# Moving eleven of the sixteen sums behind the gradient of b2 into three units of the first pass

## The chip, the cores and the metric

The kernel runs on one core of a Trainium2 chip. The core's engines are TensorE (PE, the matmuls), VectorE (DVE), ScalarE (ACT), GpSimd (POOL) and SyncE (SP, which only issues transfers); each works through its own instructions in the order in which the program gives them, and semaphores tie the engines together. The metric is the device time of one execution in microseconds (us).

## The reference

A forward pass of two branches mixed by a gate, and the gradients of all its inputs but one. `x` has 2048 tokens of 1024 features, and the hidden layer of the second branch has 3584.

```python
g = sigmoid((x * gate_w).sum(-1, keepdims=True))
X = rfft2(x.astype(float32)) * (w_r + 1j * w_i)
a = irfft2(X, s=(S, D)).astype(bfloat16)
h = einsum("bsd,df->bsf", B_x, w1) + b1
r = where(h > 0, h, 0)
b = einsum("bsf,fd->bsd", r * r, w2) + b2
out = g * a + (1 - g) * b
...
_out, _vjp = jax.vjp(_f, A_x, A_w_r, A_w_i, B_w1, B_b1, B_w2, B_b2, gate_w)
return (_out, *_vjp(grad_out))
```

The gradient at the second branch's output is `db = (1 - g) * grad_out`, a matrix of 2048 tokens by 1024 features. The gradient of `b2` is the sum of `db` over the tokens. The same `db`, multiplied by `w2` turned around, gives the gradient at the hidden layer.

## The kernel before

The second branch runs in three passes. The first pass (`mlp_in`) makes the hidden layer and its gradient and writes both to memory (`h2T_scr`, `dhT_scr`). The second (`mlp_grads`) makes the gradients of `w1` and `w2`, the third (`Outputs`) the output and the gradient of `x`. Beside the first two passes runs the first branch, a transform in stages written as generators: `first_stage` (rows, then columns of the forward transform), `fft_mid` (the rest of it, the filters, their gradients, the first part of the way back), `fft_out`. The function `spread` advances them: after each step of the pass it takes as many steps of the transform as are due. In the first pass that is 1.75 per step until `fft_mid` has begun (`"mid" in later`) and 1.5 after it. So the order of the program is fixed when the kernel is built; a list scheduler then gives each engine's final order.

The first pass begins with a stretch over the first 512 of the 3584 hidden columns. After it come 23 *units*, numbered here from 0. A unit (`Unit(fp, sp)`) is 256 hidden columns by 1024 tokens. It makes its part of the hidden layer by seven products (`p1` to `p7`, line 927, four matmuls of 512 columns each, on sums that VectorE prepares: `w_sums`, line 916). VectorE and ScalarE take these apart (`rest`: line 946 on VectorE joins two products into `rT`; line 947 is ScalarE's relu; line 934 are ScalarE's copies `cu` and `u2`; line 794 squares). Each unit also does four `back_` of the unit before: eight matmuls with `w2T` and `dbT` into a bank `pd` (line 826), and one VectorE instruction that makes `dhT` from it (line 830). The PSUM banks of `pd` and `pZ` come from one pair, those of `ph` from another; a product can start only when VectorE or ScalarE has read the one before last out of its bank. The transform's banks come from a third pair (tag `ps2`).

A unit has four steps, each ended by a `yield`: the first with `p1`, a `back_` and `p5`, the second with `p6` and a `back_`, the third with `p7` and a `back_`, the fourth with a `back_`, `p4`, `p3` and the next unit's `p2`.

The transform's lines that the text names: the first stage folds on VectorE (lines 272 to 284), matmuls `pk` (293) and `pu` (325), and joins `u` (312, 313); the middle stage reads `z` from memory (line 404, issued by ScalarE, and 402), mirrors it (`pm`, `z`, 426), multiplies matrices `px` (435), copies `x` (443 to 445), multiplies by the filter `tt` (453), joins `y` (458), makes the filter's gradient `g`, `gs` (500, 501; `gw`, 505), and goes back through `pv` (472) and `pc` (488, 489). POOL brings the filter into order (`w`, 410 to 417) and issues most stores. Before the middle stage's first product, the lines at the edges are made by `edges_through`: `parted` (357), `pe`, `ed` (366 to 370), `sp`, `ex` (382).

`dbT` holds `db` with the features on the partitions: eight chunks of 128 features, each with its 2048 tokens along the row. A sum over the tokens is a VectorE reduction along the row; `sum_of_db(n)` (line 991) does one half of one chunk, 1024 tokens, and there are sixteen of them. Each is placed behind the latest `dhT` instruction in VectorE's order (`later["last"]`), without a semaphore. `grad_of_b2` adds the two halves (line 996), turns the result by one PE transpose (line 998) into a `ps2` bank, copies it (line 1000) and stores it (line 1001). Before the change, units 1 to 16 make one sum each, in their fourth step, and unit 17 calls `grad_of_b2`.

Of the kernel before, what the change touches and what calls it, by code (L numbers as in the profile page):

```python
# [141 lines left out]
def kernel(  # L142
# [30 lines left out]
    S2, DC, FC = g.S2, g.DC, g.FC  # L173
# [76 lines left out]
    def after(ins, earlier, wait=mybir.DependencyClass.Sync):  # L250

        if earlier is not None:
            info = mybir.DependencyInfo(wait, mybir.DependencyReason.DATA)
            tc.add_manual_dep(ins.ins, earlier.ins.name, info, reason="paced")
# [514 lines left out]
    def mlp_in():  # L769
# [52 lines left out]
        def grads(fc, sb, ss, rT, dhT):  # L822
            w_ = w2T[fc // FGC]
            pd = d_bank("pd")
            for ec in range(DC):
                turn["PE"] = mm(  # L826
                    pd[:], lhsT=w_[:, ec, fc % FGC * P : (fc % FGC + 1) * P], rhs=dbT[:, ec, ss],
                    start=(ec == 0), stop=(ec == DC - 1),
                )
            return STT(  # L830
                out=dhT, in0=pd[:], scalar=2.0, in1=rT, op0=ALU.mult, op1=ALU.mult,
                accum_out=gb1part[:, fc, sb : sb + 1],
            )

        def load_w2(fg, earlier=None, halves=(0, FGW // 2)):

            if fg not in w2T:
                w2T[fg] = wb.tile([P, DC, FGW], BF16, name="w2T", tag="w2T", bufs=2)
            for h in halves:
                f0 = fg * FGW + h  # L840
                after(turned(w2T[fg][:, :, h : h + FGW // 2], B_w2[f0 : f0 + FGW // 2, :]), earlier)
# [5 lines left out]
        def load_w1(fp):  # L847
            w1[fp] = f1.tile([P, DC, PW], BF16, name="w1f", tag="w1f") if fp == 2 else wb.tile([P, DC, PW], BF16, name="w1g", tag="w1g", bufs=2)
            ld(out=w1[fp][:], in_=w1v[:, :, fp * PW : (fp + 1) * PW])
# [6 lines left out]
        def store(scr, t_, fp, sp):  # L856
            cols2 = slice(2 * sp * SW, 2 * (sp + 1) * SW)
            st(out=scr[2 * fp : 2 * fp + 2, :, cols2].rearrange("c p s -> p c s"), in_=t_[:])  # L858
# [18 lines left out]
        def back_(fp, s, c):  # L877
            if (fp, s // 2) not in dh:
                dh[fp, s // 2], left_of[fp, s // 2] = wide("dhT"), 4
            last = grads(2 * fp + c, s, rows_(s), rTs.pop((fp, s, c)), dh[fp, s // 2][:, c, rows_(s % 2)])  # L880
            later["last"] = last
            left_of[fp, s // 2] -= 1
            if not left_of[fp, s // 2]:
                store(dhT_scr, dh.pop((fp, s // 2)), fp, s // 2)
# [23 lines left out]
        def w_sums(fp, tie=None):  # L908
            (a11, a12), (a21, a22) = w_quads(fp)
            if fp % 2:  # L910
                s_ = kept[:, NT - 2 : NT, :].rearrange("p t (n f) -> p (t n) f", f=P).rearrange("p (q n) f -> p q n f", q=4)
            else:
                s_ = wb.tile([P, 4, KH, P], FP16, name="Sw", tag="Sw", bufs=1)
            s1, s2, s3, s4 = (s_[:, n] for n in range(4))
            for out, x, y, op in ((s1, a21, a22, ALU.add), (s2, s1, a11, ALU.subtract), (s3, a11, a21, ALU.subtract), (s4, a12, s2, ALU.subtract)):
                after(V(out=out, in0=x, in1=y, op=op), later["last"] if tie else None, mybir.DependencyClass.NoSync)
                yield
            S_[fp] = {1: s1, 2: s2, 3: s3, 4: s4}
# [70 lines left out]
        def sum_of_db(n):  # L989
            ec, h = divmod(n, 2)  # L990
            summed = nc.vector.reduce_sum(out=gb2[:, ec, h : h + 1], in_=dbT[:, ec, h * S // 2 : (h + 1) * S // 2], axis=mybir.AxisListType.X)
            after(summed, later["last"], mybir.DependencyClass.NoSync)

        def grad_of_b2():
            whole = wb.tile([P, DC], BF16, name="gb2b", tag="gb2b")
            V(out=whole[:], in0=gb2[:, :, 0], in1=gb2[:, :, 1], op=ALU.add)
            pb = fps.tile([DC, P], BF16, name="pb2", tag="ps2", bufs=2)
            nc.tensor.transpose(pb[:], whole[:], identb[:])
            row = wb.tile([DC, P], BF16, name="gb2r", tag="gb2r")
            nc.vector.tensor_copy(out=row[:], in_=pb[:])  # L1000
            st(out=out_7.rearrange("(c p) -> c p", p=P), in_=row[:])
# [31 lines left out]
        def freed_rows(n, low, high):  # L1033
            if n == freed + 1:
                again(slice(2 * low, 2 * low + 2), later["last"])
            elif n == len(seq) - 1 and high:
                again(slice(6 + 2 * high, 8 + 2 * high))

        units_ = [Unit(*u) for u in seq]
        first = [(i, k) for i in range(2) for k in range(2)]  # L1040
        units_[0].p2()
        for n, u in enumerate(units_):
            fg, pr = divmod(u.fp, NPR)
            if (u.fp, u.sp) == (LAST - 2, 1):
                load_w1(LAST)
            elif u.sp == 0 and u.fp < LAST - 1:
                load_w1(u.fp + 1)
            u.p1()
            if n:
                units_[n - 1].square(0, u.copy)  # L1050
            back_(*waiting[0])
            u.p5()
            freed_rows(n, 0, 1)
            if first and u.sp and "mid" in later and u.fp >= FC // 4:
                turned_group(0, *first.pop(0), later["last"])
            yield
            next(more_sums, None)
            u.p6()
            freed_rows(n, 1, 2)
            if n:  # L1060
                units_[n - 1].square(1, u.copy)
            back_(*waiting[1])
            next(more_sums, None)
            follows = u.fp + 1 if u.sp == 1 and u.fp < LAST - 2 else {(LAST - 2, 0): LAST - 1, (LAST - 1, 1): LAST}.get((u.fp, u.sp))
            ahead_ = w_sums(follows, True) if follows else iter(())
            dealt = ahead_ if (u.fp, u.sp) != (LAST - 2, 0) else iter(())
            next(dealt, None)
            yield
            u.p7()
            back_(*waiting[2])  # L1070
            next(more_sums, None)
            next(dealt, None)
            freed_rows(n, 2, 0)
            yield
            back_(*waiting[3])
            for _ in ahead_:
                pass
            next(more_sums, None)
            if pr == 0 and u.sp == 0:
                later["blocks"] = later["last"]  # L1080
            if 0 < fg < FG - 1 and pr == 0 and u.sp == (fg > 2):
                load_w2(fg + 1, later["last"])
            if 0 < n <= 2 * DC:
                sum_of_db(n - 1)
            elif n == 2 * DC + 1:
                grad_of_b2()
            u.p4()
            freed_rows(n, 3, 3)
            u.p3()
            if n + 1 < len(units_):  # L1090
                units_[n + 1].p2()
            yield
            waiting = [(u.fp, 2 * u.sp + j, c) for c, j in ((0, 0), (0, 1), (1, 1), (1, 0))]
# [14 lines left out]
    def group(n):  # L1108
        return later["odd" if n % 2 else "even"][:].rearrange("p (t f) -> p t f", t=NT)

    def turned_group(n, i, k, earlier):
        scr, fg = (h2T_scr, dhT_scr)[n // FG], n % FG
        rows_ = scr[:].rearrange("c p s -> (c p) s")[fg * FGW + i * FGW // 2 : fg * FGW + (i + 1) * FGW // 2]
        tiles, f_ = slice(k * NT // 2, (k + 1) * NT // 2), slice(i * FGW // 2, (i + 1) * FGW // 2)
        after(turned(group(n)[:, tiles, f_], rows_[:, k * S // 2 : (k + 1) * S // 2]), earlier)

    def again(rows_, earlier=None):
        after(ld(out=dbn[:, rows_, :], in_=db_scr[:, rows_, :]), earlier)
# [703 lines left out]
    warm(7)  # L1822

    units = mlp_in()
    rows_of_x(0, 2)
    vrow = f1.tile([FC + DC, P], BF16, name="vrow", tag="vrow")
# [143 lines left out]
```

## Time and profile before

| | us |
|---|---|
| median of 3 runs (1190.86 to 1193.34) | 1192.29 |
| the profiled execution, its own time | 1196.52 |
| its span, first to last instruction | 1194.7 |
| PE busy | 1173.5 |
| VectorE busy | 897.9 |
| ScalarE busy | 531.0 |
| POOL busy | 387.9 |
| the 16 sums of line 991, together | 19.4 |

The sums start at 111.5, 128.6, 147.2, 161.4, 178.8, 195.8, 209.8, 223.2, 238.8, 253.9, 268.5, 283.7, 298.7, 313.4, 330.0 and 345.1 us. They last 1.205 to 1.216 us each, and none of them has VectorE idle in front of it. The first pass's last products lie at about 455 us. The clock granted to PE is 1.00 in every stretch.

In the views shown below, a line of the timeline has the start in us, the duration, the engine, the line of the kernel, the operation, what it writes and reads, its shape, and how many instructions are merged in it; in brackets stand the idle time of the engine before it and what ended that. In a table of stretches, a row has the stretch, its length, and for each engine the busy time and the number of instructions, then PE's clock, the share of the transfer engines and GB/s. "issue" is idle time for which the profile shows no wait.

### The profile page before, as it was taken

The page shows a single profiled execution, that of the slowest core. Times are in us where ns is not written, and L with a number is a line of the kernel's source. Part 1 is how long each engine was busy: PE and PEld are TensorE (multiplying, and loading weights), DVE is VectorE, ACT ScalarE, POOL GpSimd, SP SyncE. Part 2 cuts the span into 40 slices and gives each one's busy share as a digit, 9 for nine tenths or more (in the row PEclk, how much of TensorE's full clock was granted, in tenths as well). Part 3 has the DMA queues.
Part 4 walks back from the last instruction along what each step waited for, and adds up shares of the span by engine and source line. Part 5 has one row for each costly group of instructions (what it writes and reads, how often), then busy time and mean ns, then how long its engine had stood idle before and what let it go on. Part 6 is the DMA issues. An engine that isn't in the chain of part 4 may idle for free.

```text
span 1194.7 us, 19383 instructions
## 1 busy us (share of the span) xinstructions
PE 1173.5 (98%) x7181; PEld 640.3 (54%) x7275; DVE 897.9 (75%) x1598; ACT 531.0 (44%) x961; POOL 387.9 (32%) x618
## 2 busy tenths in 40 slices
PE   8999999999999999999999999999999999999998
PEld 5555555444433444444446999998544444444444
DVE  6898887788988797877537666676786777976757
ACT  5678788577676773445224665664210010000000
POOL 0233443556666683764231333221001100000000
PEclk9999999999999999999999999999999999999999
DMA  9997675687979879889997999995889998564530
GB/s 264 287 306 215 187 203 167 196 219 180 206 186 198 253 250 184 200 187 219 208 198 165 238 226 251 243 216 153 258 188 267 238 277 272 176 194 149 180 124 36
DMA packets 329464, 249.84 MB, mean 209 GB/s; under 512 B 187912, under 2 KB 287658, under 8 KB 328858
## 3 DMA queue, kind: packets, MB, share of 16 engines
q1 hardware_dynamic: 268352, 112.12, 45.1%
q0 software_dynamic: 35136, 111.72, 29.6%
q10 hardware_dynamic: 25882, 24.76, 7.1%
q8 instruction: 57, 0.93, 0.3%
q14 instruction: 37, 0.30, 0.1%
HBM read 114.82 MB, written 89.67 MB: 171 GB/s over the span
## 4 chain that ended last, share of the span: by engine, by line
PE 69%; DVE 16%; DMA 5%; ACT 4%; issue 4%; POOL 1%; SPq 1%; ACTq 0%; another core or an unknown queue 0%; DVEq 0%; POOLq 0%
PE pX L1256 15%; PE xX L1557 14%; PE pV L1256 11%; PE pd L826 8%; PE xV L1557 7%; PE ph L927 4%; PE xZ L1557 3%; PE ph L819 2%; DVE rT L946 2%; DVE dhT L830 1%; DVE tt L453 1%; PE pui L325 1%; PE pki L634 1%; DMA z<-z_scr 1%; PE pu L325 1%
## 5 line engine op out<-in xcount | busy, mean ns | idle before, releaser
L826 PE MATMUL pd<-dbT,w2T 128*128 128x512 bf16 x860 | 206.5, 379 | 7.8 <-DVE rT L946 2.5
L826 PEld LDWEIGHTS <-w2T 128*128 128x128 bf16 x896 | 86.3, 98 | 110.4 <-issue 10.3
L1557 PEld LDWEIGHTS <-dS 128*128 128x128 f16 x686 | 66.4, 98 | 79.4 <-issue 3.8
L830 DVE SCALAR_TENSOR_TENSOR dhT<-pd,rT 128x512 bf16<-128x512 f32 x112 | 76.6, 684 | 31.6 <-PE pd L826 29.2
L1608 POOL DMA_DIRECT2D out_dram<-ot x32 | 17.4, 544 | 248.6 <-DVE ot L1664 128.0
L1674 ACT ACTIVATE w2br<-w2br,dsc 128x512 f32<-128x512 bf16 x8 | 5.8, 723 | 178.6 <-DVE ot L1664 117.4
L1557 PE MATMUL xX<-oT,dS 128*128 128x512 f16 x336 | 76.4, 379 | 0.6 <-DVE eR L1586 0.5
L1272 ACT COPY u<-pX 128x512 f32<-128x512 f32 x56 | 32.8, 586 | 90.8 <-PE pX L1256 85.2
L1557 PEld LDWEIGHTS <-odd 128*128 128x128 bf16 (+1 forms) x462 | 44.8, 98 | 51.5 <-issue 0.9
L1557 PEld LDWEIGHTS <-even 128*128 128x128 bf16 (+1 forms) x448 | 43.6, 98 | 52.6 <-issue 0.7
L1256 PEld LDWEIGHTS <-T 128*128 128x128 f16 x672 | 64.6, 98 | 7.5 <-issue 0.2
L947 ACT ACTIVATE rT<-rT 128x512 bf16<-128x512 bf16 x69 | 43.4, 629 | 50.2 <-DVE rT L946 49.8
L794 ACT ACTIVATE h2T<-rT 128x1024 bf16<-128x1024 bf16 x56 | 59.6, 1064 | 0.2
L1276 DVE TENSOR_TENSOR whi<-pV,u 128x512 bf16<-128x512 f32 x28 | 19.3, 689 | 47.1 <-ACT u L1272 47.0
L1256 PEld LDWEIGHTS <-S 128*128 128x128 f16 x336 | 32.5, 98 | 40.8 <-DVE S L1188 1.9
L491 POOL DMA_DIRECT2D y_scr<-pc x64 | 47.2, 738 | 18.1 <-DVE pc L488 11.1
L453 DVE TENSOR_TENSOR tt<-x,w 128x1028 f16<-128x1028 f16 (+1 forms) x64 | 42.6, 699 | 10.5 <-ACT x L445 4.5
L1256 PEld LDWEIGHTS <-resL 128*128 128x128 bf16 x448 | 43.1, 98 | 4.9
L1256 PEld LDWEIGHTS <-resR 128*128 128x128 f16 (+1 forms) x448 | 42.9, 98 | 4.9 <-issue 0.2
L1276 DVE TENSOR_TENSOR wlo<-pV,u 128x512 bf16<-128x512 f32 x28 | 19.2, 687 | 32.0 <-PE pV L1256 31.9
L858 POOL DMA_DIRECT2D h2T_scr<-h2T x28 | 20.9, 746 | 66.9 <-ACT f L285 29.2
L239 POOL DMA_DIRECT2D r<-y_scr x48 | 28.0, 588 | 41.9 <-ACT re L613 33.1
(382 smaller groups left out, 2798.0 us busy)
## 6 DMA issues: line engine op xcount, KB each, us to landing
h2T_scr<-h2T POOLq DMA_DIRECT2D x28, 512.0 KB, 4.3
dhT_scr<-dhT POOLq DMA_DIRECT2D x28, 512.0 KB, 6.0
y_scr<-pc POOLq DMA_DIRECT2D x64, 128.0 KB, 4.3
ax_scr<-yo POOLq DMA_DIRECT2D x16, 512.0 KB, 5.1
out_dram<-ot POOLq DMA_DIRECT2D x31, 256.0 KB, 3.7
z<-z_scr ACTq DMA_DIRECT2D x60, 128.0 KB, 4.2
out_dram<-whi POOLq DMA_DIRECT2D x28, 256.0 KB, 4.9
out_dram<-wlo POOLq DMA_DIRECT2D x28, 256.0 KB, 5.6
```

The lines of the kernel that those rows point to most:

```text
L239: st(out=a, in_=b) if stored else st(out=b, in_=a)
L453: V(out=tt[:, k, :, :, 0:W], in0=x[:, a : a + 2, :, 0:W], in1=by, op=ALU.mult)
L491: st(out=columns_of(y_scr, c, h), in_=pc[:, n])
L794: after(nc.scalar.activation(h2T, rT, ACT.Square), behind_, mybir.DependencyClass.NoSync)
L826: turn["PE"] = mm(pd[:], lhsT=w_[:, ec, fc % FGC * P : (fc % FGC + 1) * P], rhs=dbT[:, ec, ss], start=(ec == 0), stop=(ec == DC - 1),)
L830: return STT(out=dhT, in0=pd[:], scalar=2.0, in1=rT, op0=ALU.mult, op1=ALU.mult, accum_out=gb1part[:, fc, sb : sb + 1],)
L927: turn["PE"] = mm(acc[:], lhsT=lhs[:, t, :], rhs=rhs[:, t, :], start=start and t == 0, stop=t == KH - 1, skip_group_check=True,)
L947: nc.scalar.activation(rT, rT, ACT.Relu)
L1256: self.mm = mm(out, lhsT=lhs[:, t, m * P : (m + 1) * P], rhs=rhs[:, t, :], start=start and t + a == 0, stop=t == KH - 1, skip_group_check= ...
L1272: turn["ACT"] = nc.scalar.copy(out=t_[:], in_=self.X[:])
L1276: turn["DVE"] = self.added = V(out=self.half(row, j), in0=self.sums(acc), in1=self.sums(t_), op=ALU.add)
L1557: ins = mm(acc, lhsT=lhs[:, fc, :], rhs=rhs[:, fc, :], start=start and fc == 0, stop=fc == KH - 1 and bias is None, skip_group_check=True,)
```

## The change

A list holds the sixteen sums that are left, and `db_sum` makes the next one where its condition holds. The fourth step of a unit makes one from unit 1 on, as before; the first three steps make one each from unit 6 on. So units 1 to 5 make one sum each, units 6 and 7 four each, unit 8 the last three, in its first three steps. `grad_of_b2` is called at the head of the fourth step of unit 10 in place of unit 17. First stage and middle stage of the transform meet in units 7 and 8. What is computed stays the same.

```diff
+        db_left = list(range(2 * DC))
+
+        def db_sum(now):
+            if now and db_left:
+                sum_of_db(db_left.pop(0))
+
         units_[0].p2()
         for n, u in enumerate(units_):
...
             if first and u.sp and "mid" in later and u.fp >= FC // 4:
                 turned_group(0, *first.pop(0), later["last"])
+            db_sum(n >= 6)
             yield
             next(more_sums, None)
             u.p6()
...
             next(dealt, None)
+            db_sum(n >= 6)
             yield
             u.p7()
             back_(*waiting[2])
...
             freed_rows(n, 2, 0)
+            db_sum(n >= 6)
             yield
+            if n == 10:
+                grad_of_b2()
             back_(*waiting[3])
...
-            if 0 < n <= 2 * DC:
-                sum_of_db(n - 1)
-            elif n == 2 * DC + 1:
-                grad_of_b2()
+            db_sum(n > 0)
             u.p4()
```

In the order that the scheduler makes of it, the eleven sums stand on VectorE between the `dhT` instructions of units 6, 7 and 8, and `grad_of_b2`'s transpose on PE stands after the first `pv` of the middle stage and ahead of the `px` that follows it. PE's order differs by a few matmuls passed by others; from the end of the sums' old places on, the engines' orders are the same as before. On SP's queue one load of `w1g` stands ahead of two transposing loads of `w2T` that it stood behind.

## The prediction

> **What bounds the kernel now.** First the page's busy times, then a table of stretches cut at the sums of line 991, then TensorE's own pauses, the chain of waits, and the order in which VectorE works around one sum. I number the units from 0 as the loop does; unit n made sum n-1 in its fourth step, so the stretch that ends at a sum's start is one unit.
>
> ```profile
> span 1194.7 us, 19383 instructions
> ...
> PE 1173.5 (98%) x7181; PEld 640.3 (54%) x7275; DVE 897.9 (75%) x1598; ACT 531.0 (44%) x961; POOL 387.9 (32%) x618
> ```
>
> TensorE (PE) looks full, but a matmul's record is longer (0.38 us) than the step between two (eight pd in 1.73 us in the chain of waits, 0.216 each), so this share hides pauses. The stretches show who is short of time:
>
> ```profile
> core 0: us, PE busy (x) PEld busy (x) DVE busy (x) ACT busy (x) POOL busy (x), PEclk, DMA share, GB/s
> 178.82:195.84 17.02, 16.91 (x122) 9.63 (x123) 13.72 (x31) 13.87 (x28) 5.84 (x11) 1.00 0.58 186
> 195.84:209.78 13.94, 13.89 (x92) 7.45 (x91) 8.59 (x21) 11.29 (x21) 4.43 (x9) 1.00 0.48 142
> 209.78:223.17 13.39, 13.29 (x82) 6.17 (x83) 7.86 (x23) 6.25 (x10) 7.59 (x13) 1.00 0.91 286
> ...
> 283.69:298.70 15.01, 14.59 (x74) 6.17 (x70) 13.38 (x31) 12.66 (x23) 8.62 (x15) 1.00 0.85 184
> 298.70:313.41 14.71, 14.61 (x74) 6.22 (x75) 14.44 (x28) 11.70 (x21) 9.65 (x14) 1.00 1.22 191
> ```
>
> The first three rows are units 6, 7 and 8: VectorE (DVE) idles 3.30, 5.35 and 5.53 us there. The last two are crowded units of the transform's middle stage, where it idles 1.63 and 0.27. There PE does pause, each time for VectorE:
>
> ```profile
> 259.24 1.89 PE L826 MATMUL pd<-dbT,w2T 128*128 128x512 bf16 x8 [0.40 <-DVE rT L946]
> 288.93 1.89 PE L826 MATMUL pd<-dbT,w2T 128*128 128x512 bf16 x7 [0.37 <-DVE dhT L830]
> 318.88 1.89 PE L826 MATMUL pd<-dbT,w2T 128*128 128x512 bf16 x8 [0.60 <-DVE rT L946]
> 329.47 1.02 PE L826 MATMUL pd<-dbT,w2T 128*128 128x512 bf16 x4 [0.71 <-DVE dhT L830]
> 340.00 1.89 PE L826 MATMUL pd<-dbT,w2T 128*128 128x512 bf16 x8 [0.66 <-DVE dhT L830]
> 350.57 1.89 PE L826 MATMUL pd<-dbT,w2T 128*128 128x512 bf16 x8 [0.51 <-DVE dhT L830]
> ```
>
> Between 111 and 240 us PE's matmuls have one such pause, 0.2 us for an ACT copy. How a sum gets into one, VectorE's order shows (start, us):
>
> ```profile
> 283.69 1.21 DVE L991 TENSOR_REDUCE gb<-dbT 128x1 f32<-128x1024 bf16 x1
> 284.81 0.16 DVE L465 TENSOR_TENSOR y<-y,eh 128x4 f16<-128x4 f16 x1
> 284.89 0.74 DVE L946 SCALAR_TENSOR_TENSOR rT<-ph,b1col,u 128x512 bf16<-128x512 f32 x1
> 285.55 0.68 DVE L500 TENSOR_TENSOR g<-x 128x1024 f16<-128x1024 f16 x1
> 286.26 0.43 DVE L501 TENSOR_TENSOR gs<-g 128x512 f16<-128x512 f16 x1
> 286.97 1.31 DVE L453 TENSOR_TENSOR tt<-x,w 128x1028 f16<-128x1028 f16 x2 [0.28 <-ACT x L445]
> 288.19 0.68 DVE L830 SCALAR_TENSOR_TENSOR dhT<-pd,rT 128x512 bf16<-128x512 f32 x1
> ```
>
> Nothing idles between the sum and the tt but 0.28 us (ACT, whose work on rT also waited for the sum), so the dhT at 288.19, for which PE pauses at 288.93, comes up to 1.13 us late (283.69 to 284.81: records overlap a little, a sum costs 1.13).
>
> **The change, part by part.** *Removed:* one sum from each of units 9 to 16, 8 x 1.13 = 9.0 us of VectorE where it is 88% busy (107.4 of 121.9 us over the rows from 223.17 to 345.09). What PE gets of it: a pause of x costs x + 0.16 (record 0.38 less step 0.216), so the six cost 0.56, 0.53, 0.76, 0.87, 0.82, 0.67. The third follows VectorE's own wait of 1.45 us for a z transfer (to 317.40): a sum less only lengthens that wait, 0. The fourth and fifth come down the same late z as well as a sum: I count two thirds, 1.13. The other three, where the way back to a sum is packed, count in full: 1.76. Together 2.9 us. Bounds: the chain of waits from 225 to 350 us gives VectorE's sums 4.7% of 125 us, 5.8 us, the most. The least is in units that had no sum: from 392.27 to 437.80 three units took 45.53 us, and their matmuls need 3 x 60 x 0.216 = 38.9, plus five blocks of px or pv at 0.98 (242.79 to 243.78, 249.06 to 250.03) = 43.8: 0.58 us per unit above the floor. Seven units with a sum (239.97 to 346.53) took 106.56 against 7 x 60 x 0.216 + 11 x 0.98 = 101.5: 0.73 per unit. Difference 0.15 x 8 = 1.2 us. I take 2.9, the count of real pauses, between 1.2 and 5.8.
>
> A rule speaks against the full gain. The rows: all sums take 1.205 to 1.216 us, in crowded units too, while the g product of line 500 is 0.69 in the median of eleven from 231 to 337 us and 1.07 at 275.00 and 336.48. The Trainium skill (SBUF — State Buffer, Who interferes with whom) says that a reduce never contends with GpSimd for their shared port, and a two-input product does. By that the removed sums were the stretches in which POOL had the port free, and each product moved up may be stretched by 0.38: 8 x 0.38 = 3.0 of the 9.0 us, and the gain would be 2.9 x 6/9 = 1.9. The rows agree that sums aren't stretched; that the products would be is not shown.
>
> *Added:* three sums in unit 6, three in 7, two in 8 (they hold four, four, three, one each before): 3.39, 3.39 and 2.26 us into idle 3.30, 5.35, 5.53. Unit 6 is the tight one. In the order in which the built kernel issues, three sums come between the dhT at 182.53 and the rT<-ph,b1col,u at 196.97; the gaps before it are 0.36, 0.47 and 1.23 = 2.06, so this rT ends 1.33 us later, at about 198.96 instead of 197.63. It frees the bank into which p5 of unit 7 starts at 198.59: PE pauses 0.37. Behind it wait rT<-pZ (198.30) and a dhT, but the next dhT waits for PE until 203.21 (3.57 us idle), which takes the rest. Unit 7's sums fall into this gap and the 1.05 and 2.75 us at 212.83 and 217.13, unit 8's partly into 2.75 and 0.84; the small product `parted` (220.33) of the edge lines then starts about 1.2 us later, but its consumer tt stands idle 1.96 us at 227.96, and PE's order puts px behind the same pZ as before: 0. Loss 0.4 us; bounds 0 and 3.6 (rival below).
>
> *Moved:* grad_of_b2 from unit 17 to unit 10: 0.15 and 0.20 us of VectorE, one transpose that cost PE 0.42 (357.82), one bank of the pair ps2 between a pv and the next px, one small store on POOL's queue. Same count, same kind of place: 0, bounds -0.4 and +0.4. On SP's queue one load of w1g passes ahead of two transposing loads of w2T, all for units two or more later (they landed in 6.5 and 10.7 us, a unit is 15): 0. The change adds no DMA and no wait; behind the sums, VectorE's order holds dhT and rT, whose banks PE waits for, which is counted above.
>
> *Sum:* -2.9 + 0.4 = -2.5 us. The profiled execution took 1196.5 us (span 1194.7 and 1.8 around it), so 1194.0; it stands 4.2 above the median of 1192.29, and the forecast for the median is **1189.8**. After 346 us the passes stand in PE's order in long chains and start from where this pass ends, so I carry the gain to the end in full.
>
> **The rivals.**
> *The chain is right:* all sums on it come off, 5.8 - 0.4: 1186.9. For: VectorE's lines fill that chain. Against: much of it runs beside a PE that is fed, and only 5.1 us above the floor exist from 239.97 to 346.53.
> *PE and the transfers set the pace anyway:* units without sums took 45.53 / 3 = 15.18 us, with sums 106.56 / 7 = 15.22. Then 1.2 - 0.6 (0.37 and 0.25 for a px that does wait): 1191.7. For: the z transfers land late (9.29 us before 317.40) and come no sooner. Against: the later units had troubles of their own, a pause of 1.51 at 381.69 behind a wn transfer of 10.4.
> *Unit 6 can't take its sums (slower):* its idle pieces are waits for PE and ACT, and sums that sit ahead of data just arriving do not fill them. Then rT is 3.39 late, p5 of unit 7 waits 201.02 - 198.59 = 2.4, and the 1.2 of `parted` reach px too: 3.6, less the 1.2 of the rival before: 1194.7. It decides from the point where PE pauses over 2.9 us between 190 and 226. For: 13.72 + 3.39 = 17.1 in a unit of 17.02. Against: the gap of 3.57 right behind it.
> That the sums stay where they were is excluded by the order of the built kernel.
>
> **How the numbers follow.** The forecast's case gets 0.50, the chain 0.14, no bound by sums 0.19, unit 6 0.17. A measurement here can tell about 0.2% (2.4 us) from no change; of the forecast's case (about -1 to -4) I put six tenths beyond it. Faster 0.50 x 0.6 + 0.14 = 0.44; within 0.50 x 0.4 + 0.19 = 0.39; slower 0.17. The range reaches from somewhat under the chain's time, 1186.5, to 1194.2, which leaves out most of unit 6's case; the forecast's own is 1188.3 to 1191.3.
>
> **What would show it.** Eleven reduces between about 183 and 222 us, none after; PE's pauses for rT and dhT from 238 to 350 down from 2.7 us to under 1; the sum of units 9 to 16 about 3 us shorter; one pause of under 0.5 us near 198. Wrong, if unit 6 grows by over a microsecond, if the pauses stay with other releasers (z, ACT), or if the first pass ends earlier and the kernel does not.

## The result, and the profile after

The changed kernel takes 1203.88 us in the median of six runs (1198.68 to 1206.86), the kernel before 1193.13 in the six beside and ahead of them (1190.86 to 1195.45). The ratio is 1.0072, with a 95 % interval of 1.0049 to 1.0094: slower by 8.6 us by that ratio (0.0072 of 1193) where 2.5 us less was forecast, and outside the range. The profiled execution took 1206.86 us.

First the head of the page, then TensorE's timeline, its pauses alone:

```profile
span 1205.1 us, 19475 instructions
...
PE 1181.2 (98%) x7275; PEld 640.7 (53%) x7275; DVE 896.6 (74%) x1598; ACT 530.1 (44%) x961; POOL 386.8 (32%) x618
```

```profile
258.01 1.89 PE L826 MATMUL pd<-dbT,w2T 128*128 128x512 bf16 x8 [1.53 <-DVE dhT L830]
266.43 3.57 PE L927 MATMUL ph<-dbn 128*128 128x512 f16 x8 [6.53 <-DVE rT L946]
...
332.63 3.32 PE L826 MATMUL pd<-dbT,w2T 128*128 128x512 bf16 x8 [3.18 <-DVE rT L946]
344.79 1.02 PE L927 MATMUL ph<-xT,w1g 128*128 128x512 bf16 x4 [0.63 <-DVE rT L946]
```

The six short pauses shown in the prediction are gone. Three longer ones stand in their stead, and two short ones (0.63 us, shown, and 0.23 us at 302.95). The eight matmuls behind the longest took 3.57 us instead of 1.89: the clock granted from 266.4 to 270 us was 0.50. The page's totals show nothing of this; VectorE is even 1.3 us less busy.

To find the place, I took from each timeline where the line `rT<-ph,b1col,u` of a unit's fourth step starts; the distance of two is a unit.

| end of unit | before, us | after, us | after minus before |
|---|---|---|---|
| 5 | 179.95 | 180.28 | 0.33 |
| 9 | 239.97 | 240.68 | 0.71 |
| 10 | 255.01 | 265.63 | 10.62 |
| 14 | 314.55 | 324.74 | 10.19 |
| 15 | 331.14 | 344.00 | 12.86 |
| 19 | 392.27 | 403.44 | 11.17 |
| 22 | 437.80 | 448.55 | 10.75 |

From the end of unit 5 to that of unit 9, where the sums now are, the time grew by 0.4 us. Unit 10 grew by 9.9. It has no sum; `grad_of_b2` now stands in its last step, but it does so too in the first kernel of the experiments, whose unit 10 takes 14.9 us. VectorE's timeline in unit 10, after the change:

```profile
256.93 0.43 DVE L426 TENSOR_TENSOR pm<-z 128x512 f16<-128x512 f16 x1 [3.76 <-DMA z<-z_scr]
...
264.68 0.42 DVE L426 TENSOR_TENSOR pm<-z 128x512 f16<-128x512 f16 x1 [6.39 <-DMA z<-z_scr]
265.63 0.74 DVE L946 SCALAR_TENSOR_TENSOR rT<-ph,b1col,u 128x512 bf16<-128x512 f32 x1
```

VectorE stands 10.15 us for two `z` transfers. The `rT` behind it in its order frees the bank for which PE waits 6.53 us. So the next question is why `z` is late. Two views answer it: SP's timeline, and the transfers issued from 236 to 256 us (queue, count, KB each, median us from issue to landing, of those whose landing is recorded). Before, then after:

```profile
238.27 7.38 SPq L183 DMA_TRANSPOSE w2T<-in_B_w_dram  x2
245.77 0.51 SPq L849 DMA_DIRECT2D w1g<-in_B_w_dram  x1
```

```profile
238.56 0.37 SPq L849 DMA_DIRECT2D w1g<-in_B_w_dram  x1
239.78 13.09 SPq L183 DMA_TRANSPOSE w2T<-in_B_w_dram  x2
```

```profile
dhT_scr<-dhT POOLq DMA_DIRECT2D x2, 512.0 KB, 5.0
z<-z_scr ACTq DMA_DIRECT2D x4, 128.0 KB, 4.7
...
w2T<-in_B_w_dram SPq DMA_TRANSPOSE x2, 8.3
```

```profile
w1g<-in_B_w_dram SPq DMA_DIRECT2D x1, 512.0 KB, 4.2
dhT_scr<-dhT POOLq DMA_DIRECT2D x1, 512.0 KB, 12.4
z<-z_scr ACTq DMA_DIRECT2D x4, 128.0 KB, 13.3
...
w2T<-in_B_w_dram SPq DMA_TRANSPOSE x2, 13.2
```

Three times from the end of unit 9 on, a pair of transposing `w2T` loads and a `w1g` load stand side by side on SP's queue; I call these the late pairs. The first late pair now stands behind its `w1g`, and the `z` loads and the `dhT` store beside it, on two other queues, take 12 to 13 us in the median instead of 5. It is not that more is moved. The table of stretches over the same 15 us, before, after, and in a kernel of a later section that has load and pair as after the change, but in which the `dhT` store is held some 10 us and the loss is gone (the last two columns are the time that the packets took, as a share of the 16 transfer engines' time, and GB/s; over 1.00, packets overlap on an engine):

```profile
243.00:258.00 15.00, 14.89 (x75) 6.44 (x74) 11.53 (x25) 13.12 (x23) 7.88 (x13) 1.00 1.00 256
```

```profile
243.00:258.00 15.00, 13.49 (x69) 5.41 (x67) 7.23 (x19) 11.64 (x21) 3.96 (x7) 1.00 1.24 147
```

```profile
243.00:258.00 15.00, 15.00 (x77) 6.24 (x76) 10.99 (x27) 13.43 (x24) 7.60 (x12) 1.00 0.94 240
```

After the change the packets take more of the engines' time, 1.24 for 1.00, though only 147 GB/s are moved for 256. The third row moves 240 GB/s in a share of 0.94: so after the change the packets take longer for the same bytes. The load itself has landed by 242.8 us (238.56 and 4.2), ahead of this stretch; pair, store and `z` stay slow behind it.

### The profile page after: what moved, and what is told of

The parts are those of the page before. It is cut to its first block, busy times and chain, and to the rows that moved or that the text cites. A ratio compares the mean times of both kernels' runs of the same rounds, so it can differ in the third digit from the quotient of the medians.

```text
span 1205.1 us, 19475 instructions
## 1 busy us (share of the span) xinstructions
PE 1181.2 (98%) x7275; PEld 640.7 (53%) x7275; DVE 896.6 (74%) x1598; ACT 530.1 (44%) x961; POOL 386.8 (32%) x618
## 4 chain that ended last, share of the span: by engine, by line
PE 75%; DVE 13%; DMA 4%; ACT 4%; issue 3%; POOL 1%; ACTq 0%; SPq 0%; DVEq 0%; POOLq 0%
PE pX L1264 15%; PE xX L1565 14%; PE pV L1264 11%; PE pd L826 9%; PE xV L1565 7%; PE ph L927 5%; PE xZ L1565 4%; DMA z<-z_scr 3%; PE ph L819 2%; PE pui L325 1%; DVE rT L946 1%; PE pki L634 1%; DVE dhT L830 1%; DVE tt L453 1%; PE pu L325 1%
## 5 line engine op out<-in xcount | busy, mean ns | idle before, releaser
L826 PE MATMUL pd<-dbT,w2T 128*128 128x512 bf16 x896 | 212.0, 382 | 5.2 <-DVE rT L946 3.2
L1284 DVE TENSOR_TENSOR whi<-pV,u 128x512 bf16<-128x512 f32 x28 | 19.3, 688 | 47.1 <-ACT u L1280 47.1
L515 POOL DMA_DIRECT2D out_dram<-gw x64 | 33.8, 534 | 24.2 <-ACT eh L463 16.2
```

The costliest lines, as they stand in the source:

```text
L515: st(out=every(dst_w, k), in_=gw[lanes[n], c_, 0:W1])
L826: turn["PE"] = mm(pd[:], lhsT=w_[:, ec, fc % FGC * P : (fc % FGC + 1) * P], rhs=dbT[:, ec, ss], start=(ec == 0), stop=(ec == DC - 1),)
L1284: turn["DVE"] = self.added = V(out=self.half(row, j), in0=self.sums(acc), in1=self.sums(t_), op=ALU.add)
```

## The experiments

Each kernel was timed in turn with the kernel before on the same chip. Its ratio is to those runs.

### Is it the order on SP's queue?

Three theories stood at the start. *Order*: the `w1g` load that passed ahead of the pair. *Timing*: the moved sums shift `z` or the pair, whatever the order. *Sums*: the sums cost time in their new units. In the first two kernels only SP's order differs from their base; PE, VectorE, ScalarE and POOL have the base's. (In the diffs, `...` stands for lines left out; small helpers are left out too.)

The changed kernel with that one load tied behind the pair:

```diff
-                after(turned(w2T[fg][:, :, h : h + FGW // 2], B_w2[f0 : f0 + FGW // 2, :]), earlier)
+                later["turned"] = turned(w2T[fg][:, :, h : h + FGW // 2], B_w2[f0 : f0 + FGW // 2, :])
+                after(later["turned"], earlier)
...
-            ld(out=w1[fp][:], in_=w1v[:, :, fp * PW : (fp + 1) * PW])
+            load = ld(out=w1[fp][:], in_=w1v[:, :, fp * PW : (fp + 1) * PW])
+            if fp == 8:
+                after(load, later["turned"], mybir.DependencyClass.NoSync)
```

> The changed kernel, but the w1g load for 256 columns number 8 stands behind the first of the three late pairs of transposing w2T loads on SP's queue again, as it did before the change; every other engine's order is that of the changed kernel. Theory ORDER (the load that passed ahead makes the pair land in 13 and 20 us in place of 8.3, and the z load behind it 15.8 in place of 4.7, which is the stall of 9.9 us in unit 10): unit 10 takes about 15 us again, z lands in under 7 us, and the time is that of before or up to 2.5 us under it, 1190 to 1194. Theory TIMING (the z loads come at a worse moment against the pair because the sums are gone, in whichever order SP issues): within 2 us of the changed kernel, about 1203. Theory SUMS (the sums in units 6 to 8 cost the time): 1203.

1192.86 us, ratio 1.0000 (0.9981 to 1.0019). All of the loss is gone. The transfers of the same stretch:

```profile
z<-z_scr ACTq DMA_DIRECT2D x4, 128.0 KB, 5.6
...
w2T<-in_B_w_dram SPq DMA_TRANSPOSE x2, 8.1
```

The reverse, the kernel before with this pair behind that load:

```diff
+                if u.fp == 7:
+                    load_w2(4, later["last"], behind_=later["w1"])
...
-            if 0 < fg < FG - 1 and pr == 0 and u.sp == (fg > 2):
+            if 0 < fg < FG - 1 and fg != 3 and pr == 0 and u.sp == (fg > 2):
```

> The kernel before, with nothing changed but that the first of the three late pairs of w2T loads stands behind that w1g load on SP's queue. ORDER: slower by 8 to 11 us (1201 to 1204), with a z load of over 12 us near 250 to 265 and PE pauses of over 5 us there. TIMING and SUMS: within 2 us of the kernel before (1191 to 1195).

1197.93 us, ratio 1.0053 (1.0031 to 1.0076), without a sum moved. Its `w2T` took 12.0 us and the four `z` of unit 10 took 11.4, and unit 10 grew from 15.0 to 20.7 us in the profile. So Order is shown from both sides and Timing and Sums fall, though the loss is less than expected, and its runs spread over 9.6 us. (The profiled execution, 1203.97 us, also lost 6.9 us ahead of unit 0, before the swapped load; that isn't the swap's.)

The second and third late pair stood behind a `w1g` load in the kernel before already. Two kernels put the pair ahead of the load there as well (`fp in (8, 10, 12)` in the first diff), on the changed kernel and on the one before:

> The changed kernel with all three late w2T pairs ahead of the w1g load that follows them. ORDER: all three pairs land in 8 to 9 us each, the stalls of unit 15 (2.7 us) and unit 17 vanish too: 1187 to 1191. If the pairs are slow for another reason: no better than the run with only the first pair restored.

> The kernel before with the second and third late w2T pair ahead of the w1g load (the first already is). ORDER: the pauses of 0.60 at 318.9 and 1.51 at 381.7 us vanish, 1188 to 1192. TIMING: same as before, 1191 to 1195.

1193.35 us, 1.0006 (0.9983 to 1.0029), and 1196.93 us, 1.0027 (1.0010 to 1.0043). Order expected a gain, and there was none. The waits of TensorE from 340 to 400 us in the second say why (in the first the same wait is 1.9 us):

```profile
PE pZ L930 <- DMA w1g<-in_B_w_dram: 4.2, 1, 4.2
```

Behind the third pair, `w1g` itself came too late for the unit that needs it. What the pair no longer held up, the load did.

### What about the order does it?

*Queue*: a pair is slow when a plain load stands right ahead on its queue. *Late*: the load pushes the pair 4 us back onto the `z` loads. *Bytes* or *overlap*: the two must not be in flight together. The four kernels here ran on a chip on which the kernel before itself took 1199.58 us (1191.96 to 1205.87), so their ratios are less sharp than their profiles.

The pair 4 us later, `w1g` behind it:

```diff
             back_(*waiting[0])
+            if (u.fp, u.sp) == (7, 0):
+                load_w2(4, later["last"])
+                load_w1(8)
```

> The changed kernel with the w1g load of unit 10 again behind the two transposing loads of w2T on SP's queue, but both tied to the first dhT of unit 10 instead of the last of unit 9, some 4 us later; the orders of the five engines are those of the version with the order restored (1192.9 us). QUEUE (a transposing pair is slow, and makes others slow, when a plain load stands right ahead of it on its own queue): the pair lands in 7 to 9 us, the four z of unit 10 in 5 to 7, 1191 to 1195 us. LATE (the w1g load does harm only because it pushes the pair 4 us back, onto the z loads and the stores of h2T and dhT): z lands in 9 to 16 us as in the changed kernel, VectorE waits 5 to 10 us for it, 1199 to 1204 us.

1197.69 us, 0.9978 (0.9956 to 1.0000). The pair set out at 243.32 us, with the `z` loads; `z` landed in 5.0 us in the median, and unit 10 took 15.1 us. Late falls.

The load on GpSimd's queue (`st` for `ld` where `fp == 8`):

> The changed kernel with this one w1g load issued from GpSimd's queue instead of SP's, at the same point of the program, so that the pair of w2T has nothing ahead of it on SP's queue while the same bytes move at the same time. QUEUE: pair in 7 to 9 us, z in 5 to 7, 1191 to 1195 us. LATE or BYTES (it is 512 KB more in flight at this time, by whatever queue): z in 9 us or more, 1197 to 1204 us; so too if the issue on GpSimd's queue holds up the wn loads and the dhT store behind it, which the timeline of POOL would show as later issues there.

1219.92 us, 1.0175 (1.0132 to 1.0219): the worst of all, and more than any theory gave. The transfers issued from 236 to 256 us:

```profile
z<-z_scr ACTq DMA_DIRECT2D x6, 128.0 KB, 24.7
w1g<-in_B_w_dram POOLq DMA_DIRECT2D x1, 512.0 KB, 11.5
dhT_scr<-dhT POOLq DMA_DIRECT2D x1, 512.0 KB, 14.1
...
w2T<-in_B_w_dram SPq DMA_TRANSPOSE x2, 22.5
```

Nothing stands ahead of the pair on its own queue here, and its two loads take 16.5 and 28.5 us (22.5 in the median). Queue falls in this form. The `dhT` store was not held up: it was issued at 246.18 us, as unit 9 ended (246.12).

The pair some 10 us later, behind a `w1g` load that has landed:

> The changed kernel with the w1g load ahead of the pair, as it is, but the pair tied to the third dhT of unit 10, some 10 us later: the w1g load has landed by then and so have most of the four z. QUEUE in its strict form (what stands ahead on the queue makes the pair slow): pair in 11 to 14 us, and what is issued in that time (h2T and dhT stores, y_scr, out_dram) lands in 9 us or more; 1192 to 1200 us, by what waits for these. OVERLAP (a pair and the plain transfers slow each other only while they are in flight together): pair in 6 to 9 us, z in 3 to 5, no wait for z in unit 10: 1190 to 1194 us.

1199.13 us, 1.0010 (0.9984 to 1.0036). `w1g` landed in 4.4 us, `z` in 2.4, and unit 10 took 14.7 us: no harm in that place. On this chip the next pair costs instead; VectorE waited 6.28 us for a `z` in unit 15.

Without the eight sums of the crowded units (reading two tokens, each takes 0.15 us instead of 1.21):

> The changed kernel with the order of the w1g load restored (1192.9 us), in which the eight sums 8 to 15 of db (those that the change moves out of the crowded units) read two tokens instead of 1024: they take some 0.06 us instead of 1.2, so that neither the old places nor the new ones pay for them. FREE (the sums set no pace where they were nor where they are): within 1 us of both the kernel before and of the version with the order restored, 1191.5 to 1193.5 us. PREDICTION (removal from units 9 to 16 is worth 2.9 us, and their new places cost 0.4): 2.9 under the kernel before, 1189.3 to 1190.5 us, and 0.4 under the version with the order restored. SUMS (the new places cost what the old ones gained, 2 to 3 us): 2 to 3 us under both, 1189.5 to 1190.5 us.

1199.66 us, 1.0001 (0.9976 to 1.0026). It is not under the kernel before, as Free has it, but with this spread it decides little. The question comes again below.

### With all three pairs out of the way

The load and the pair apart in all three places:

```diff
             back_(*waiting[2])
...
+            if 2 < fg < FG - 1 and pr == 1 and u.sp == 0:
+                load_w2(fg + 1, later["last"])
...
-            if 0 < fg < FG - 1 and pr == 0 and u.sp == (fg > 2):
+            if 0 < fg < FG - 1 and pr == 0 and u.sp == (fg > 2) and fg < 3:
                 load_w2(fg + 1, later["last"])
```

Side by side on one chip: the changed kernel again, the changed kernel with this move, the kernel before with it, and the changed kernel with it and without the eight sums.

> The changed kernel as it is, beside the three below on one chip, since the kernel before has had medians of 1192.6 and 1199.6 us in two calls on two chips. All theories that put the loss down to transfers: slower than before by 5 to 11 us on the chip where before takes 1192 to 1193; on one where before takes 1199 or more, before itself has lost time to the later pairs, and the difference is 0 to 8 us.

1199.85 us, 1.0043 (1.0016 to 1.0070), beside 1192.60 for before: slower again, by 7.3 us.

> The changed kernel with the last three pairs of transposing loads of w2T all tied to the third dhT of the unit behind, some 10 us later, each still behind its w1g load on SP's queue but when that has landed; nothing else moves on any engine. OVERLAP (a pair and a w1g load in flight together make every transfer slow, and this alone makes z late): w1g in 4 to 5 us, z in 2.5 to 5, no wait of VectorE for z over 1 us in the units 10, 15 and 18, 3 to 8 us less than the kernel before of the same call (3 where before takes 1192 to 1193, 8 where it takes 1199 or more). PAIR (a pair slows whatever is beside it; later it only meets other transfers, even and the next z): waits for z or even of 3 us and more in the unit behind, within 2 us of before.

1190.61 us, 0.9979 (0.9965 to 0.9994), the runs from 1190.11 to 1193.00. VectorE waits for no `z` in the first pass. The gain over the kernel before is 2.0 us, where *Overlap* asked for 3.

> The kernel before with the same move of the three pairs: it differs from the version of the changed kernel with this move in the sums of db and grad_of_b2 alone, and both have the same order on SP's queue. OVERLAP: as that one, 3 to 8 us under before. Of the sums: PREDICTION says that it takes 2.5 us more than the changed kernel with the move, FREE that the two agree within 1 us, SUMS that it takes 2 us or more less.

1191.39 us, 0.9985 (0.9970 to 1.0001), with the sums in their old places: 1.2 us under the kernel before, not quite clear of no change.

> The changed kernel with the three pairs moved, in which the sums 8 to 15 of db read two tokens instead of 1024. FREE: within 1 us of the changed kernel with the move. PREDICTION: 0.4 us less than that (the price of the new places), which can't be told from FREE here, and 2.9 less than the kernel before with the move. SUMS: 2 us or more less than the changed kernel with the move.

1191.07 us, 0.9981 (0.9968 to 0.9994).

The three agree within 0.8 us: where the sums stand, and whether they are made, can't be told from the time. What gain there is comes of three pairs of loads, and needs no sum moved. TensorE's pauses between 235 and 350 us in its timeline, first with the sums in their old places, then with them moved:

```profile
287.17 1.89 PE L826 MATMUL pd<-dbT,w2T 128*128 128x512 bf16 x8 [0.36 <-DVE dhT L830]
336.82 1.89 PE L826 MATMUL pd<-dbT,w2T 128*128 128x512 bf16 x8 [0.66 <-DVE dhT L830]
347.40 1.89 PE L826 MATMUL pd<-dbT,w2T 128*128 128x512 bf16 x8 [0.51 <-DVE dhT L830]
```

```profile
291.88 1.02 PE L927 MATMUL ph<-xT,Sw 128*128 128x512 f16 x4 [0.24 <-ACT u L934]
328.72 1.02 PE L927 MATMUL ph<-xT,w1g 128*128 128x512 bf16 x4 [0.40 <-DVE rT L946]
```

### Which transfers don't go together?

Two theories were left. *Ahead*: `w1g` ahead makes the pair slow by itself. *Crowd*: it only holds up pair and `dhT` store until both run beside `z`. The base has the second and third pair moved away and the first as the change puts it.

> The changed kernel with only the second and third of the late pairs moved some 10 us later (with all three moved: 1190.6 us, 1190.1 to 1193.0); the first stands as the change puts it, right behind the w1g load of unit 10. All theories that put the loss into this one place: 5 to 11 us over the version with all three moved, all of it in unit 10, 1195 to 1202 us. If the loss were in the later pairs too, it would be less than 4 us.

1198.80 us, 1.0052 (1.0033 to 1.0071): 8.2 over the version with all three moved, which ran on another chip (the kernel before took 1192.75 us here and 1192.60 there). Nearly the whole of it is in unit 10, which is 7.6 us longer.

The same with the `dhT` store held some 10 us:

```diff
             if not left_of[fp, s // 2]:
-                store(dhT_scr, dh.pop((fp, s // 2)), fp, s // 2)
+                if (fp, s // 2) != (6, 0):
+                    store(dhT_scr, dh.pop((fp, s // 2)), fp, s // 2)
...
             back_(*waiting[2])
...
+            if (u.fp, u.sp) == (7, 0):
+                store(dhT_scr, dh.pop((6, 0)), 6, 0, later["last"])
```

> As the version in which only the second and third pair are moved, but the store of dhT that stands on GpSimd's queue beside the first pair is held some 10 us, to the third dhT of unit 10. CROWD (w1g ahead does harm because it holds up the 512 KB dhT store and the pair, so that pair, store, z and the store of h2T are all in flight together): without the store the pair lands in 6 to 9 us and z in 5 to 7, under 1194 us. AHEAD (a plain load right ahead of a pair makes the pair slow by itself): pair 11 to 14 us, z over 9 as before, 1195 to 1202 us.

1190.95 us, 0.9975 (0.9956 to 0.9994). All gone, with the load still right ahead of the pair. The transfers of 236 to 256 us with the store beside the pair, then with it held:

```profile
w1g<-in_B_w_dram SPq DMA_DIRECT2D x1, 512.0 KB, 4.6
z<-z_scr ACTq DMA_DIRECT2D x4, 128.0 KB, 11.3
h2T_scr<-h2T POOLq DMA_DIRECT2D x1, 512.0 KB, 13.0
...
w2T<-in_B_w_dram SPq DMA_TRANSPOSE x2, 12.4
```

```profile
w1g<-in_B_w_dram SPq DMA_DIRECT2D x1, 512.0 KB, 4.3
z<-z_scr ACTq DMA_DIRECT2D x4, 128.0 KB, 4.0
h2T_scr<-h2T POOLq DMA_DIRECT2D x1, 512.0 KB, 3.8
...
w2T<-in_B_w_dram SPq DMA_TRANSPOSE x2, 6.3
```

Ahead falls: the pair takes half the time. Crowd has two kernels of its own, the pair 4 us later with `w1g` behind it (as above), and the same with the store tied to that point too:

> The version with all three pairs moved, but the first of them tied to the first dhT of unit 10 (some 4 us behind the end of unit 9), with its w1g load behind it: the pair starts as the z loads do, the dhT store has landed by then. Both CROWD and AHEAD: z in 4.5 to 6 us, within 2 us of the version with all three moved, 1190 to 1193 us. LATE (the pair being pushed onto the z loads is the harm): 1195 us or more.

> As the version with the first pair tied to the first dhT of unit 10 and w1g behind it, but the dhT store is tied to the same dhT, so that pair, dhT store, z and soon the h2T store set out together with no w1g load ahead. CROWD: pair 11 us or more, z in 8 us or more, 1194 to 1202 us. AHEAD: pair in 6 to 9, z in 4.5 to 7, 1190 to 1193 us.

1191.00 us, 0.9985 (0.9962 to 1.0007), and 1191.69 us, 0.9985 (0.9971 to 0.9998). In the second the pair, the store and the first two `z` set out within about 1 us of each other, which is all that Crowd asks for, and yet:

```profile
z<-z_scr ACTq DMA_DIRECT2D x4, 128.0 KB, 7.0
...
w2T<-in_B_w_dram SPq DMA_TRANSPOSE x2, 9.2
```

Unit 10 is 1.7 us longer, not 7. So Crowd falls as the whole cause too. What is left is that load, pair and store are all three in flight. In the last run the load is ahead, as in the base, and the store starts when it has landed:

> The version in which only the second and third pair are moved and the first stands right behind its w1g load (1198.8 us; 1190.95 with the dhT store held 10 us), with the dhT store held only 4 us, to the first dhT of unit 10: it then sets out when the w1g load has landed (242.5 us), but with the pair and the z loads. THREE (any two of w1g load, pair and dhT store go together, all three at once do not): the store lands in 6 to 8 us, z in 5 to 8, unit 10 at most 2 us longer, 1190.5 to 1193.5 us. AHEAD AND CROWD (a plain load ahead of the pair on the queue, and a store beside the pair, whenever the store starts): store in 10 us or more, z in 9 or more, 1196 to 1201 us.

1190.54 us, 0.9978 (0.9964 to 0.9992), no loss in the time. The profile lies between: `z` took 8.4 us in the median and the store 8.8, more than was expected of *Three*, and unit 10 grew by 2.5 us, of which the next gave back 1.4. When the three set out, in us, with `z`'s median and the length of unit 10, of one profile each (the load took 4.3 to 4.6 us where it went first):

| kernel | load | pair | `dhT` store | `z` | unit 10 |
|---|---|---|---|---|---|
| all three pairs moved | 237.96 | 250.14 | 239.78 | 2.2 | 14.59 |
| store held 10 us | 238.24 | 239.49 | 250.70 | 4.0 | 14.61 |
| pair and store 4 us later, load behind | 250.89 | 242.98 | 243.25 | 7.0 | 16.30 |
| store held 4 us | 237.99 | 239.34 | 243.80 | 8.4 | 17.06 |
| first pair as the change puts it | 237.81 | 238.96 | 239.51 | 11.3 | 22.18 |

In the first four rows at most two of the three are in flight at a time, in the last all three. So at the first late pair *Three* fits every run: any two together are harmless or cost up to 2.5 us in unit 10, the three together 5 to 10, and 18 where the load was on GpSimd's queue. At the second late pair, where the store sets out some 3 us behind the load, it is not a matter of yes and no: unit 15 takes 14.3 to 15.2 us in the eight profiles with that pair moved away, 15.3 to 19.3 in the five in which it stands behind its load, and 20.8 to 26.0 in the four on the chip with the slower kernel before. How much the three overlap seems to set the price; that was not measured. The overlap is short, too: in the last row of the table the load has landed by 242.4 us, 2.9 us after the store set out, and before the first `z` does (243.56 us), and yet `z` is slow. Why three should be so much worse than two, and why it outlasts the load, is open as well; the trace shows the busy share and the rate, not what the packets wait for.

## Why the prediction was wrong, step by step

*The step that failed* is in the part on what is moved: "On SP's queue one load of w1g passes ahead of two transposing loads of w2T, all for units two or more later (they landed in 6.5 and 10.7 us, a unit is 15): 0." It asked only whether the moved transfers would be in time for their own readers. They were. It did not ask what else is in flight beside them and who waits for that: the `dhT` store, and through it and the pair the `z` loads, which VectorE needs within a few microseconds. That step cost 7 to 9 us, the whole result: 7.8 by the medians with the other two pairs moved away (1198.80 less 1191.00, where the first pair sets out 4 us later, ahead of its load), 7.3 for the changed kernel beside the kernel before (1199.85 less 1192.60), and 8.6 by the ratios with and without the swap (1.0072 and 1.0000). The trace of before held the control: of its three late pairs, the one ahead of `w1g` landed in 8.3 us with `z` at 4.7, and the two behind a `w1g` load landed in 12.8 to 14.2 us with `z` at 8.5 to 10.9. The 10.7 us that the prediction took for the pair is the median over the first two pairs together, one in each order (8.3 twice, 13.0 and 13.8), and so hid the difference. The prediction even quoted such a `z` (9.29 us) and did not ask what stood beside it.

*The gain in the crowded units*, 2.9 us from six pauses, was too large. With the transfers out of the way and the sums in their old places, three of the six remain (288.93, 340.00 and 350.57 of before, now 0.36, 0.66 and 0.51) and go when the sums move: these were the sums'. The other three (259.24, 318.88, 329.47) go without a sum moved. They were counted in one execution, 4.2 us above the median, in which VectorE waited 0.39 and 1.45 us for `z` ahead of the first two. In the changed kernel with the order restored VectorE has no such wait, and these two are gone there too, so a late `z` had a part in them; whether a sum had one as well is not shown. The prediction had counted the first in full, the third at two thirds, and only that at 318.88 at 0. By its own price (x + 0.16) the three that were the sums' are 2.0 us, and three shorter ones that stand there when the sums are moved (0.24, 0.40, and 0.24 at 351.20) take back 1.4. From the end of unit 9 to that of unit 22 the version with moved sums takes 192.30 us (240.12 to 432.42), the other 193.10 (238.50 to 431.60), 0.8 less. VectorE did get what was forecast: it is busy for 163.55 us of that stretch instead of 172.50, 8.95 less, and eight sums at 1.13 are the forecast's 9.0. The term that was too large is TensorE's share of it, 0.8 in place of 2.9.

*The loss in the units that take the sums*, 0.4, was right in size by luck: 0.4 in the changed kernel, and 0.59 with the pairs moved (unit 5 to unit 9, 60.33 against 59.74 us). The pause of TensorE for VectorE near 198 us that was to show it is not there. Another one is, in unit 6, for ScalarE, in every profile with moved sums and in none without. Here ScalarE, then TensorE, in the changed kernel with the pairs moved:

```profile
188.44 0.21 ACT L285 COPY f<-f 128x4 f16<-128x4 f16 x1 [0.27 <-DVE f L284]
```

```profile
188.70 0.62 PE L293 MATMUL pk<-kg,f 128*128 128x128 f16 x8 [0.35 <-ACT f L285]
```

The first moved sum, at 182.98 us, stands ahead of VectorE's folds, of which line 283 now starts 7.85 us behind the end of unit 5 (187.64) instead of 6.55 (185.31 less 178.76). The prediction looked only at `rT` and the bank behind it. By its price this pause costs 0.5 us.

So gain and loss nearly cancel, and the medians, 1190.61 and 1191.39, differ by less than a measurement can tell. Of the rivals, that TensorE and the transfers set the pace anyway is the one that the runs bear out for the sums. Unit 6 grew by 0.92 us, just under the microsecond that was to speak against the prediction, and part of it came back by the end of unit 9; the chain was not worth 5.8.

*The rule of the Trainium skill* (SBUF — State Buffer, Who interferes with whom) was used to have the products that move up take back 3.0 of the 9.0 us. The runs show nothing of that size: 8.95 of the 9.0 us are gone from VectorE's busy time, and the products of line 500 take 0.70 us at most between 231 and 337 us with the sums moved, where two took 1.07 before. That a reduce is not stretched agrees with the trace in the new places too (1.207 to 1.215 us).

*grad_of_b2* moved at no cost that any profile shows: with the pairs out of the way TensorE has no pause in unit 10. It was not tried alone.

*What was named as a sign*: the eleven sums stood where they were forecast, at 183.47 to 221.08 us, but TensorE's pauses for `rT` and `dhT` from 238 to 350 us did not fall from 2.7 us to under 1: they rose to 11.9 (1.53, 6.53, 3.18 and 0.63). The releasers were VectorE's `dhT` and `rT` as before, and VectorE in its turn waited for `z`. "The pauses stay with other releasers (z, ACT)" comes nearest to what happened, for a reason that was not among the rivals. None of them was a transfer made slow by an order that the change did not write: a scheduler chose it.

## What to carry to other kernels

An edit to one engine can make a scheduler reorder another's queue, and there the whole effect may lie: compare the order of every queue, and for each transfer that changes place ask what is in flight beside it and which of these is waited for soonest, not only whether it is itself in time. Before pricing such a swap, look in the trace for the same pair of transfers in the other order; a kernel that repeats a stage often holds both. Large transfers that nothing waits for soon belong in the stretch after the urgent ones have landed: here that was worth 1.2 us with the sums in their old places and 2.0 with them moved, of which only the second is clear of no change. The runs of these two spread over 6.7 and 2.9 us (twelve each), those of the kernel before over 9.9 (31).

## What the runs showed of the hardware

A pair of transposing loads of 512 KB each (by the kernel's shapes), a plain load of 512 KB and a store of 512 KB got in one another's way far beyond their bytes: in the 15 us after all three had been in flight at once the packets took a share of 1.24 of the 16 transfer engines' time to move 147 GB/s, and 0.94 to move 240 GB/s where the store had been held. The Trainium skill (Advanced Engine Details and Errata, X-Bar Transpose (TRN2)) says that transposing transfers are as fast as plain ones on this chip. The runs don't show that, though none of them has one alone: in the kernel with the store held, the plain load took 4.3 us and the transposing load right behind it 6.3, for the same 512 KB, and in company a transposing load took up to 14.2 us in the kernel before and 28.5 in that with the load on GpSimd's queue.

The kernel before did not take the same time wherever it was measured: 1192.6 to 1192.9 us in the median on four chips, 1199.6 on a fifth, where all four kernels profiled took 20.8 us or more for unit 15, at the second of the late pairs (15.3 to 19.3 elsewhere with that pair behind its load).

After a long stall TensorE was slow for a while. The eight matmuls behind the pause of 6.53 us took 3.57 us instead of 1.89, at a granted clock of 0.50 from 266.4 to 270 us; behind the pauses of 3.18 us (changed kernel), 4.05 (the changed kernel on another chip) and 5.38 (only the second and third pair moved) eight took 3.32, 3.45 and 3.44. Behind pauses of 1.53 and 1.94 us they took 1.89.
